# A planner's model of one PSUM bank: when a transposition into the shared bank counts as ready

## The chip, the cores and the metric

The kernel runs on one core of a Trainium2 chip. The metric is the device time of one execution in microseconds (us); the runs shown are executions of the same program. PE is TensorE, DVE is VectorE, ACT is ScalarE, POOL is GpSimd, SP is SyncE.

## The reference, cut to what matters

Three layers follow each other on the same 3072 tokens of width 512.

```
x  = attention(q, k, v)            # 4 x 8 heads, 768 tokens, local window of 96 and 8 global keys
x  = x + gate * moe(x)             # tokens with x @ w_skip > 0; expert = argmax(x @ w_gate); probability as gate
    h = max(x[mask] @ w1[e], 0);  y[mask] = gate * (h @ w2[e])       # 8 experts, 512 -> 1024 -> 512
out = moe2(x)                      # each expert takes at most 384 tokens, greedily over all sorted logits
    for idx in argsort(-logits.flatten()): take the token for the expert if both are still free
    h = max(x[mask] @ w1[e], 0);  out[mask] = h @ w2[e]
```

## The kernel before

After the attention (until about 238 us) come two series of expert products. In the first, one unit is one expert with 256 token slots (two blocks of 128), eight units, and one extra unit for an expert with too many tokens. In the second, one unit is one expert with 384 slots (three blocks), again eight units. Before a unit's products its token rows are gathered from memory by slot numbers (tile xg), turned block by block by four 128x128 transpositions on PE into the PSUM tile pt (`x_turn`, line 1044), copied by ACT as the rounded half xh, and subtracted on DVE for the remainder xl (`x_low`, line 1054). A product is done as three rounded ones (xh with wh, xl with wh, xh with wl). `mm1` (line 1058) makes ph = x @ w1 for one eighth of the hidden width, 12 matmuls; ACT and DVE make hh and hl of it; `mm2` (line 1083) adds h @ w2 into py, 9 matmuls in the second series. Weights come from memory (wr), ACT rounds them (wh), POOL or DVE subtracts (wl).

All tiles named pt share one PSUM bank: the pool `fps` (line 1022) has one buffer per name. Five places write one: the turns of x, the epilogue of the first series (`tr`, line 1281, which turns the result rows x2), the extra unit (`extra_rest`, line 1469), and two small products of the slot numbers (`slots`, line 1686: pb and pi).

Beside the expert products run generators, called streams: the turns of the next unit ("x"), the routing of the second layer ("main", which finds a threshold by counting in rounds of DVE comparisons gm and PE products pr), its slot numbers ("ids"), and the extra unit ("extra"). The program is written out in one order per engine while it is built, and that order is chosen by a model of the engines, `Clock` (line 20): each instruction written is given a start and an end from the model's costs, and the model remembers who wrote and read which part of each tile. A stream yields the engine it goes on with and the tiles that it reads. Before each expert matmul `hook` (line 1151) asks each stream in order of rank whether it is ready by the time PE gets there:

```
t = max(ck.at["pe"] + T_EPS, ck.ready("pe", (), aps))
for s_ in order():
    if s_.when() <= t:
        s_.step()
```

`when` (line 1141) is the model's time at which the tiles to be read are written. `wait_for` (line 1162) steps the streams until a condition holds, where nothing else is to be written. In `x_stream` (line 1178) the subtraction of a turn is put on a list (`lows`) and written to DVE when xh is there in the model (`flush`, line 1174); the next turn is asked for right after that. A unit's start waits for all its turns (`split2`, line 1195). "x" has rank 3 until the routing is more than a unit ahead, then rank 0, "main" 2 and then 1, "ids" 0.5 and then 2, "extra" 4.

In the model a DVE subtraction of 128x512 costs 0.067 + 512/960 us, and a result of DVE reaches PE 0.15 us after its end. Line 123 is the helper through which all instructions are written, so all carry it in the profile.

Of the kernel before, what the change touches and what calls it, by code (L numbers as in the profile page):

```python
# [7 lines left out]
F32 = mybir.dt.float32  # L8
# [153 lines left out]
def tile_attn_moe_moe(ctx: ExitStack, tc: tile.TileContext, q, k, v, n_global, n_local,  # L162
# [12 lines left out]
    KC = Dm // 128  # L175
# [348 lines left out]

    WWT, WWN = 1, (2, 5)
    T_GAP, T_SP, T_EPS, T_W, T_P, T_L, T_F, X_B, T_H, T_M, LEAN, T_G, DIRECT, CUT = 0, 0.65, 0.1, 0, 8, 1, 0.3, 3, -4, 0, 2, 1, 13, 16
    ck.late = T_G
    W_ = Weights()

# [324 lines left out]
    class Unit:  # L854
        at, tb, py, defer, xh = None, 0, 0, None, None
# [10 lines left out]
    for e in range(E):  # L866
        U_ = Unit()
# [154 lines left out]
    fps = ctx.enter_context(tc.tile_pool(name="fps", bufs=1, space=bass.MemoryType.PSUM))  # L1022
# [4 lines left out]
    bank = fps.tile([128, 512], I32, name="bank")  # L1027
    bank_at = [192]

    def in_bank(n, dt=F32):  # L1030
        bank_at[0] += n
        return bank[:, bank_at[0] - n:bank_at[0]].bitcast(dt)
# [8 lines left out]
    raw_p, fe_p = in_bank(NT), in_bank(NT)  # L1041
    fo_p = in_bank(2 * E).rearrange("p (a e) -> p a e", a=2)

    def x_turn(U_, tb, bank="pt"):
        if tb == 0 and not U_.xh:
            U_.xh = ff.tile([128, KC, width], F32R, name="xh")
            U_.xl = ff.tile([128, KC, width], F32R, name="xl")
        p = fps.tile([128, KC, 128], F32, name=bank)
        for c in range(KC):
            nc.tensor.transpose(p[:, c], U_.xs[tb][:, c * 128:(c + 1) * 128], ident)  # L1050
        U_.xt[tb] = p
        nc.scalar.activation(U_.xh[:, :, tb * 128:(tb + 1) * 128], p, AF.Copy)
# [75 lines left out]
    class Stream:  # L1128
# [11 lines left out]

        def when(self):
            eng, aps = self.need
            t = ck.ready(eng, (), aps)
            return max(t, ck.at["dve"] - T_SP) if eng == "dve" else t

# [26 lines left out]
    lows = []  # L1172

    def flush():
        while lows:
            lows.pop()()

    def x_stream(U_):
        for tb in range(len(U_.xs)):
            yield "pe", [U_.xs[tb]]  # L1180
            x_turn(U_, tb)
            lows.append(lambda tb=tb: x_low(U_, tb))
            yield "dve", [U_.xh[:, :, tb * 128:(tb + 1) * 128]]
            flush()
            U_.tb += 1
# [82 lines left out]
    def epi1(U_, tasks):  # L1268
        nb = len(U_.xs)
        if U_.defer is not None:  # L1270
            if U_.defer == 0:
                tasks.append(lambda: gate2(U_))
                tasks.append(lambda: gate2_rows(U_))
                tasks.append(table)
                tasks.extend([lambda: None] * 3)
                tasks.append(table_clear)
            return
        rows2(U_)
        U_.x2t = fx_.tile([128, KC, 256], F32, name="x2t")

        def tr(tb):
            flush()
            p = fps.tile([128, KC, 128], F32, name="pt")
            for c in range(KC):
                nc.tensor.transpose(p[:, c], U_.x2[tb][:, c * 128:(c + 1) * 128], ident)
            nc.scalar.activation(U_.x2t[:, :, tb * 128:(tb + 1) * 128], p, AF.Copy)

        def lg():
            p = fps.tile([128, 256], F32, name="pr")
            n = nb * 128  # L1290
            for c in range(KC):
                nc.tensor.matmul(p[c * 32:(c + 1) * 32, :n], wg2[:, c, :], U_.x2t[:, c, :n], start=True, stop=True)
            U_.ls = fx_.tile([128, 256], F32, name="ls1")
            nc.scalar.activation(U_.ls[:, :n], p[:, :n], AF.Copy)

        def lt():
            p = fps.tile([128, HI, KC, 32], F32, name="pr")
            for tb in range(nb):
                nc.tensor.transpose(p[:, tb].rearrange("p c e -> p (c e)"), U_.ls[:, tb * 128:(tb + 1) * 128], ident)
            lgo = ff.tile([128, HI, E], F32, name="lgo")  # L1300
            nc.vector.tensor_reduce(lgo[:, :nb], p[:, :nb, :, :E].rearrange("p j c e -> p j e c"),
                                    axis=AX.X, op=OP.add)
            for tb in range(nb):
                scatter(l2d, U_.sid[:, tb:tb + 1], lgo[:, tb], l2_st)
            U_.tasks = None

        U_.tasks = tasks
        for tb in range(nb):
            tasks.append(lambda tb=tb: tr(tb))
        tasks.append(lg)  # L1310
        tasks.append(lt)
        if U_ is not X_:
            tasks.extend(rt_tasks[:3])
            del rt_tasks[:3]
# [20 lines left out]
    tb_rhs = rt.tile([128, NT + 3], BF, name="tb_rhs")  # L1335
# [133 lines left out]
    def extra_rest(hs_):  # L1469
        hT = []  # L1470
        for half in range(2):
            yield "pe", hs_[2 * half:2 * half + 2]
            flush()
            p = fps.tile([128, 4, 128], F32, name="pt")
            for c in range(4):
                nc.tensor.transpose(p[:, c], hs_[2 * half + c // 2][:, c % 2 * 128:(c % 2 + 1) * 128], ident)
            th = fx_.tile([128, 4, 128], F32R, name=f"th{half}")
            tl_ = fx_.tile([128, 4, 128], F32R, name=f"tl{half}")
            nc.scalar.activation(th, p, AF.Copy)
            nc.vector.tensor_tensor(tl_, p, th.bitcast(F32), op=OP.subtract)  # L1480
            hT.append((th, tl_))
            X_.turned += 1
        X_.y = [fps.tile([128, Dm], F32, name="py2")]
        for c in range(FC):
            need(NE * NCH + 4 + c // 2)
            ww = W_.parts[NE * NCH + 4 + c // 2]
            for i, (a, b_) in enumerate(P3):
                yield "pe", [hT[c // 4][a], ww[b_]]
                nc.tensor.matmul(X_.y[0], hT[c // 4][a][:, c % 4], ww[b_][:, (c % 2) * Dm:(c % 2 + 1) * Dm],
                                 start=c == 0 and i == 0, stop=c == FC - 1 and i == 2)  # L1490
            W_.free = 4 * NE + (c + 1) // 2
            W_.pump()
        while units1[NE - 1].tasks:
            units1[NE - 1].tasks.pop(0)()
        tasks = []
        epi1(X_, tasks)
        for ap, t in zip((X_.x2[0], X_.x2t, None), tasks):
            yield "pe", [ap if ap is not None else X_.ls]
            t()
# [186 lines left out]
    def slots(ph_, fe, fx):  # L1686
        ttb = rt.tile([128, 1], BF, name="ttb")
        dv.tensor_tensor_scan(fe[:, 5], fe[:, 4], wrow_p[:, :NT], 0.0, op0=OP.add, op1=OP.bypass)
        dv.tensor_copy(ttb, fe[:, 5, NT - 1:NT])
        dv.tensor_copy(tb_rhs[:, :NT], fe[:, 5])  # L1690
        yield "pe", [ttb]
        flush()
        pb = fps.tile([128, KC, 128], F32, name="pt")
        te(pb[:, 0, 0:1], tri, ttb, start=True, stop=True)
        dv.tensor_copy(fx[:, 3:4], pb[:, 0, 0:1])
        dv.tensor_tensor(fx[:, 4:5], pb[:, 0, 0:1], fe[:, 5, NT - 1:NT], op=OP.add)
        dv.tensor_scalar(tb_rhs[:, NT + 1:NT + 2], fx[:, 3:4], 256.0, None, op0=OP.min)
        ma = rt.tile([128, CAP], F32, name="ma")
        mp = rt.tile([128, CAP], BF, name="mp")
        dv.tensor_scalar(ma, islot, fx[:, 3:4], None, op0=OP.is_ge)  # L1700
        dv.tensor_tensor(tb_rhs[:, NT + 2:NT + 3], pb[:, 0, 0:1], tb_rhs[:, NT + 1:NT + 2], op=OP.subtract)
        dv.scalar_tensor_tensor(mp, islot, fx[:, 4:5], ma, op0=OP.is_lt, op1=OP.mult)
        yield "pe", [mp, tb_rhs]
        flush()
        pi = fps.tile([128, KC, 128], F32, name="pt")
        for h in range(NH):
            te(pi[:, h, :NT + 3], mp[:, h * 128:(h + 1) * 128], tb_rhs, start=True, stop=True)
        ix = rt.tile([128, 3, NH], F32, name="ix")
        cx = rt.tile([128, NH, NT], F32, name="cx")
        ids = rt.tile([128, NH], I32, name="ids", bufs=E)  # L1710
        dv.tensor_tensor(ix[:, 0], snum, pi[:, :NH, NT + 1], op=OP.subtract)
        dv.tensor_tensor(ix[:, 0], ix[:, 0], pi[:, :NH, NT + 2], op=OP.subtract)
        dv.tensor_tensor(cx, pi[:, :NH, :NT], ix[:, 0][:, :, None].to_broadcast([128, NH, NT]), op=OP.is_le)
        dv.tensor_reduce(ix[:, 1], cx, axis=AX.X, op=OP.add)
        dv.scalar_tensor_tensor(ids, pi[:, :NH, NT], float(NT), ix[:, 1], op0=OP.mult, op1=OP.add)
        result[ph_] = ids
        if ph_:
            if unit_no[0] >= ph_ - 1:
                units2[ph_].load()
# [39 lines left out]
    for p in range(E):  # L1759
        U_ = Unit()  # L1760
# [62 lines left out]
```

## Time and profile before

| what | us |
|---|---|
| median of 3 runs | 870.54 (867.64 to 871.69) |
| the profiled execution | 866.52 |
| its span, first to last instruction | 864.8 |
| PE busy (matmuls) in the span | 772.2 |
| PE weight loads busy | 629.1 |
| DVE, ACT, POOL busy | 522.2, 411.4, 422.1 |

The mean granted clock of PE is 0.959 of 2.4 GHz. In the profile a row names engine, operation, output<-inputs by tile names; "idle before" is the time in which the engine stood still just ahead of an instruction, and behind the arrow is what ended that. Ends of matmuls are modelled, since they are pipelined: one that lies in a stream of others starts before the one ahead has ended. PEld rows are the weight loads of PE.

### The profile page before, as it was taken

What the parts mean: (1) busy time and instruction counts of PE and PEld (TensorE: products, weight loads), DVE (VectorE), ACT (ScalarE), POOL (GpSimd) and SP (SyncE); (2) the same over time, 40 slices, a digit from 0 to 9 for tenths busy, and PEclk for the clock granted to TensorE, in tenths of its full rate; (3) what the DMA queues carried; (4) which work ended last, traced back from release to release, by engine and by line L of the source; (5) the groups of instructions that cost most, each with busy time, mean ns of one, the idle gap of its engine ahead of it and who ended that gap; (6) DMA issues with size and microseconds to landing.
All of it is one profiled execution on the core that took longest, in us unless ns stands there. A gap on an engine that the chain in (4) does not pass through costs nothing.

```text
span 864.8 us, 16657 instructions
## 1 busy us (share of the span) xinstructions
PE 772.2 (89%) x5711; PEld 629.1 (73%) x5711; DVE 522.2 (60%) x1896; ACT 411.4 (48%) x923; POOL 422.1 (49%) x569
## 2 busy tenths in 40 slices
PE   7999998998788899998879938998989898899994
PEld 5777776676577778787768626777778787798993
DVE  6978879795555555644443584777777777712110
ACT  5887787875465445543552123334243342435211
POOL 5554557643234335442341444566484847568411
PEclk9999999999979999998999965999999999999997
DMA  8677888877166466545550051526263443555000
GB/s 188 178 207 184 231 213 218 223 208 217 28 195 206 155 213 212 189 143 183 170 192 6 17 203 49 168 89 219 91 202 116 154 135 134 161 180 164 32 37 36
DMA packets 141013, 132.82 MB, mean 154 GB/s; under 512 B 62523, under 2 KB 107835, under 8 KB 140928
## 3 DMA queue, kind: packets, MB, share of 16 engines
q1 hardware_dynamic: 132160, 111.09, 43.1%
q0 software_dynamic: 7168, 20.26, 6.8%
q8 instruction: 46, 0.75, 0.4%
q10 hardware_dynamic: 1600, 0.39, 0.2%
q14 instruction: 39, 0.32, 0.1%
HBM read 109.55 MB, written 23.49 MB: 154 GB/s over the span
## 4 chain that ended last, share of the span: by engine, by line
PE 41%; issue 11%; DVE 9%; POOL 4%; DMA 3%; ACT 2%; POOLq 0%; SPq 0%; DVEq 0%; ACTq 0%
PE ph L123 19%; PE py L123 17%; PE pr L123 3%; DMA wr<-in_moe_w_dram 3%; PE pt L123 3%; POOL wl L123 2%; DVE bank L123 2%; ACT wh L123 1%; DVE gm L123 1%; DVE xl L123 1%; DVE wl L123 1%; POOL out_dram L123 1%; DMA xg<-xd,gid 1%; DVE hl L123 1%; DVE fr L123 0%
## 5 line engine op out<-in xcount | busy, mean ns | idle before, releaser
L123 POOL TENSOR_TENSOR wl<-wr,wh 128x1024 fp32r<-128x1024 f32 (+1 forms) x97 | 204.8, 2128 | 143.6 <-ACT wh L123 142.9
L123 ACT ACTIVATE wh<-wr 128x1024 fp32r<-128x1024 f32 (+1 forms) x148 | 141.1, 984 | 49.2 <-PE py L123 27.5
L123 ACT ACTIVATE hh<-ph 128x384 fp32r<-128x384 f32 (+2 forms) x130 | 56.7, 436 | 224.5 <-PE ph L123 202.5
L123 DVE SCALAR_TENSOR_TENSOR hl<-ph,hh 128x256 fp32r<-128x256 f32 (+1 forms) x128 | 62.3, 487 | 129.8 <-ACT hh L123 124.4
L123 PE MATMUL py<-wh,hl 128*128 128x512 f32 x320 | 129.4, 404 | 1.6 <-DVE hl L123 1.6
L123 PE MATMUL py<-wh,hh 128*128 128x512 f32 x320 | 128.6, 402 | 0.4 <-ACT hh L123 0.4
L123 PE MATMUL py<-wl,hh 128*128 128x512 f32 x320 | 128.9, 403 | 0.0
L123 POOL TENSOR_SCALAR pb<-pb,st 128x232 f32<-128x232 f32 (+1 forms) x192 | 82.4, 448 | 72.5 <-PE pP L123 25.6
L123 ACT ACTIVATE pb<-sb,st 128x232 f32<-128x232 f32 (+1 forms) x192 | 113.8, 663 | 4.8 <-DVE st L123 4.5
L123 PE MATMUL ph<-xh,wh 128*128 128x256 f32 (+1 forms) x512 | 106.0, 325 | 2.5 <-ACT wh L123 1.5
L123 PE MATMUL ph<-xl,wh 128*128 128x256 f32 (+1 forms) x512 | 102.8, 319 | 0.0
L123 PE MATMUL ph<-xh,wl 128*128 128x256 f32 (+1 forms) x512 | 102.4, 319 | 0.0
L123 PEld LDWEIGHTS ph<-xh,wh 128*128 128x128 f32 x512 | 84.4, 194 | 12.1 <-issue 2.3
L123 PEld LDWEIGHTS ph<-xl,wh 128*128 128x128 f32 x512 | 82.4, 194 | 0.2
L123 PEld LDWEIGHTS ph<-xh,wl 128*128 128x128 f32 x512 | 81.9, 194 | 0.4 <-issue 0.2
L123 DVE TENSOR_TENSOR wl<-wr,wh 128x1024 fp32r<-128x1024 f32 x51 | 64.6, 1287 | 24.3 <-ACT wh L123 23.6
L123 PEld LDWEIGHTS py<-wh,hl 128*128 128x128 f32 x320 | 60.7, 190 | 14.0 <-DVE hl L123 2.4
L123 DVE COPY pts<-pP 116x512 f32<-116x512 f32 (+1 forms) x96 | 61.0, 676 | 13.0 <-PE pP L123 12.2
L123 PEld LDWEIGHTS py<-wh,hh 128*128 128x128 f32 x320 | 60.9, 190 | 8.0 <-ACT hh L123 0.6
L123 PEld LDWEIGHTS py<-wl,hh 128*128 128x128 f32 x320 | 60.8, 190 | 8.0
L123 DVE CUSTOM_DVE_ANT_0 sb<-pS,bias 128x232 f32<-128x232 f32 (+1 forms) x192 | 61.4, 373 | 2.0 <-PE pS L123 1.4
L123 ACT ACTIVATE xh<-pt 128x512 fp32r<-128x512 f32 x38 | 22.7, 597 | 60.4 <-PE pt L123 48.4
(454 smaller groups left out, 1220.0 us busy)
## 6 DMA issues: line engine op xcount, KB each, us to landing
wr<-in_moe_w_dram SPq DMA_DIRECT2D x136, 512.0 KB
xd<-xs SPq DMA_DIRECT2D x32, 192.0 KB
x2d<-xs SPq DMA_DIRECT2D x32, 192.0 KB
kraw<-in_k_dram SPq DMA_DIRECT2D x30, 192.0 KB
qraw<-in_q_dram SPq DMA_DIRECT2D x30, 192.0 KB
vw<-in_v_dram SPq DMA_DIRECT2D x32, 160.0 KB
vw<-in_v_dram SPq DMA_DIRECT2D x32, 120.0 KB
xT<-in_moe_w_dram SPq DMA_DIRECT2D x1, 1536.0 KB
```

The costliest lines, as they stand in the source:

```text
L123: r = f(*a, **k)
```

## The change

For four of the five writers the stream now says "pt" instead of "pe". For those, `when` also asks the model for the time at which the last pt tile written has been read by all who read it, and adds 0.7 us if a subtraction that reads it has still to be written. The tile is remembered in `last_pt` by a helper `turns()`. Tile, bank, pool and the instructions themselves are as before.

```
+    T_LOW = 0.7
+    last_pt = []
+    def turns():
+        p = fps.tile([128, KC, 128], F32, name="pt")
+        last_pt[:] = [p[:, :, :]]
+        return p
     def x_turn(U_, tb, bank="pt"):
-        p = fps.tile([128, KC, 128], F32, name=bank)
+        p = fps.tile([128, KC, 128], F32, name=bank) if bank != "pt" else turns()
         def when(self):
             eng, aps = self.need
+            if eng == "pt":
+                return ck.ready("pe", last_pt, aps) + (T_LOW if lows else 0)
             t = ck.ready(eng, (), aps)
             return max(t, ck.at["dve"] - T_SP) if eng == "dve" else t
     def x_stream(U_):
         for tb in range(len(U_.xs)):
-            yield "pe", [U_.xs[tb]]
+            yield "pt", [U_.xs[tb]]
         def tr(tb):
             flush()
-            p = fps.tile([128, KC, 128], F32, name="pt")
+            p = turns()
     def extra_rest(hs_):
-            yield "pe", hs_[2 * half:2 * half + 2]
+            yield "pt", hs_[2 * half:2 * half + 2]
-            p = fps.tile([128, 4, 128], F32, name="pt")
+            p = turns()
     def slots(ph_, fe, fx):
-        yield "pe", [ttb]
+        yield "pt", [ttb]
-        pb = fps.tile([128, KC, 128], F32, name="pt")
+        pb = turns()
-        yield "pe", [mp, tb_rhs]
+        yield "pt", [mp, tb_rhs]
-        pi = fps.tile([128, KC, 128], F32, name="pt")
+        pi = turns()
```

## Rows read from the trace of the kernel before

**Rows 1.** Busy time by stage: stretch, its length, busy per engine (instructions), PEclk, DMA.
```profile
238.00:500.00 262.00, 238.21 (x1613) 201.12 (x1614) 132.66 (x263) 115.03 (x180) 98.81 (x105) 0.96 0.46 155
500.00:525.00 25.00, 8.17 (x99) 5.97 (x98) 17.91 (x60) 6.78 (x9) 9.88 (x10) 0.57 0.55 196
525.00:800.00 275.00, 259.24 (x1565) 212.68 (x1565) 177.88 (x736) 104.56 (x150) 174.63 (x113) 0.97 0.45 145
```

**Rows 2.** Waits of PE from 525 to 800 us: total, times, longest.
```profile
PE pt L123 <- DVE xl L123: 12.4, 12, 1.2
PE pt L123 <- issue: 1.7, 2, 1.2
PE pt L123 <- DVE mp L123: 1.6, 1, 1.6
```

**Rows 3.** Waits of PE from 238 to 500 us.
```profile
PE pt L123 <- DMA xg<-xd,gid: 4.9, 5, 1.3
PE pt L123 <- DVE tl L123: 4.7, 2, 3.3
PE pt L123 <- DVE xl L123: 2.9, 4, 0.9
...
PE ph L123 <- ACT wh L123: 1.5, 1, 1.5
PE pt L123 <- ACT x2t L123: 1.4, 2, 0.7
PE pt L123 <- issue: 1.1, 1, 1.1
```

**Rows 4.** Timeline of PE, 558 to 561 us: start, length, instruction [idle before].
```profile
558.32 0.39 PE L123 MATMUL py<-wl,hh 128*128 128x512 f32 x1
558.55 0.39 PE L123 MATMUL py<-wh,hl 128*128 128x512 f32 x1
560.16 0.66 PE L123 MATMUL pt<-ident,xg 128*128 128x128 f32 x4 [1.22 <-DVE xl L123]
560.65 0.30 PE L123 MATMUL pr<-oh,gm 128*128 128x32 bf16 x6
```

**Rows 5.** Timeline of DVE in the same stretch.
```profile
558.95 0.56 DVE L123 SCALAR_TENSOR_TENSOR hl<-ph,hh 128x384 fp32r<-128x384 f32 x1
559.42 0.68 DVE L123 TENSOR_TENSOR xl<-pt,xh 128x512 fp32r<-128x512 f32 x1
```

**Rows 6.** Groups of weight loads, 525 to 800: count, busy, mean ns, idle before.
```profile
L123 PEld LDWEIGHTS pt<-ident,xg 128*128 128x128 f32 x84 | 9.3, 140 | 20.1 <-DVE xl L123 17.1 <-issue 2.4
```

**Rows 7.** Groups of matmuls from 525 to 800 us, the same columns.
```profile
L123 PE MATMUL pr<-oh,gm 128*128 128x32 bf16 x180 | 9.3, 178 | 0.0
L123 PE MATMUL pr<-cs,sel 128*128 128x32 f16 x30 | 5.7, 189 | 0.0
```

**Rows 8.** Timeline of PE at the extra unit, 421 to 425.5 us.
```profile
422.73 0.39 PE L123 MATMUL ph<-xh,wh 128*128 128x256 f32 x1 [1.46 <-ACT wh L123]
...
424.97 0.68 PE L123 MATMUL pt<-ident,hh 128*128 128x128 f32 x2 [1.41 <-DVE tl L123]
```

**Rows 9.** Busy time by stage again, around the two falls of the clock.
```profile
391.00:397.70 6.70, 6.00 (x26) 5.50 (x27) 1.24 (x2) 2.11 (x5) 1.59 (x2) 0.50 0.72 243
425.00:428.40 3.40, 3.40 (x10) 2.86 (x11) 1.41 (x2) 2.29 (x3) 1.14 (x1) 0.50 0.84 247
388.00:391.00 3.00, 0.00 (x0) 0.00 (x0) 1.83 (x2) 2.04 (x3) 1.85 (x2) 0.98 1.02 391
```

**Rows 10.** Timeline at the start of unit 1, DVE and PE.
```profile
568.77 0.68 DVE L123 TENSOR_TENSOR xl<-pt,xh 128x512 fp32r<-128x512 f32 x1
...
574.39 0.86 PE L123 MATMUL ph<-xl,wh 128*128 128x384 f32 x4
```

**Rows 11.** Timeline of PE ahead of unit 0, second and third turn.
```profile
519.12 1.09 PE L123 MATMUL pt<-ident,xg 128*128 128x128 f32 x4 [1.13 <-issue]
...
522.84 1.09 PE L123 MATMUL pt<-ident,xg 128*128 128x128 f32 x4 [2.52 <-issue]
```

## The prediction, on record before the result

> **What bounds the kernel now.** I read the page's busy shares first, then the busy time by stage, then what TensorE (PE) waited for in each stage, then single instructions in order of time.
>
> The stages [rows 1] show PE busy 238.2 of 262 us in the first matrix products, and 259.2 of 275 us in the first seven units of the second. Between them lie 25 us of routing in which PE works 8.2 us. DVE is busy 178 and POOL 175 of the 275 us: neither is near full. The reader is to see that outside the short stage nothing but PE itself, and what PE stands still for, can set the time.
>
> What PE stood still for from 525 to 800 us is one thing [rows 2]: 12.4 us in 12 stops until the subtraction "xl" on DVE, 1.7 us in 2 more at the same instruction that the view puts down to issue, and 1.6 us for the routing's own "mp". So 14 stops, 14.1 us, all ahead of a transposition into the bank pt: the second and third turn of each of seven units. From 238 to 500 us the list is longer [rows 3]: at pt again 2.9 us in 4 stops for xl and 1.1 us in one; 4.7 us in 2 for "tl" (the longest 3.3); 1.4 us in 2 for the copy x2t; and 4.9 us in 5 for gathered rows that had not landed.
>
> One stop from close by [rows 4]: the py matmul starts at 558.55, the next instruction of PE, four transpositions of a second turn, at 560.16. On DVE [rows 5] hl runs from 558.95 and xl, the last reader of the bank, from 559.42 to 560.10. The planner let the turn go as soon as its rows were there; PE reached it and stood. Behind it in PE's order were matmuls with everything they need.
>
> **The change part by part.** No instruction is added or removed: it alters the moment at which a generator that is about to write pt counts as ready. Four places ask that way: a turn of x, the extra unit's two turns, and two small products of the slot numbers. The epilogue's turns (tr) only report their bank and aren't asked.
>
> *Turns in the second matrix products.* 14 stops of 14.1 us go [rows 2]. The column of idle time undercounts: the py before starts 0.23 us after its forerunner (558.32, 558.55), so PE could have gone on at 558.78; it went on at 560.16, 1.38 us later, where the column has 1.22 [rows 4]. That is 0.16 us more per stop, 14 x 0.16 = 2.2 us. Cover: mm1 and mm2 are asked before every matmul, and a unit's 168 of them in the expert products stand ready, since rows 2 show no wait of theirs. If that cover were gone, the stop would be back at 1.0 us on the mean.
>
> The weight loads of these turns stood 17.1 + 2.4 = 19.5 us [rows 6] where the matmuls stood 14.1. The Trainium skill ("Perfetto Trace Analysis", section Identifying the Most-Contended Engine) says that the busy time of matmuls is a poor measure of PE, as they are pipelined, and that weight loads are to be looked at instead. By that rule alone this stage would give 5.4 us more than the column, and the sum below 3.2 us more; the trace agrees in direction, and my size is that of the starts.
>
> *Turns in the first matrix products.* From rows 3 go xl 2.9 us, issue 1.1 us, one of the two x2t stops (a turn of x right behind a turn of tr), 0.7 us, and one of the two tl stops, the extra unit's second turn, 1.4 us: 6.1 us in 7 stops, with 7 x 0.16 = 1.1 us more. The other tl stop (3.3 us) and the other x2t stop are tr's and stay; the gathers' 4.9 us stay too, since what the planner thinks of a landing isn't altered.
>
> *Is the planner right about DVE?* If it lets the turn go too early, part of the stop stays. Lower bound nothing: other instructions that the same model lets go when DVE is done, 180 + 30 of the routing's products, show 0.0 us of idle time in all [rows 7]. Upper bound: where the model is wrong, as with the gathers, 4.9 / 5 = 1.0 us is left per stop [rows 3], which is all of it. The routing's products are nearer: same stage, same pair of engines. The formula has 0.067 + 512/960 = 0.60 us for xl and 0.15 us for the hand-over; measured are 0.68 us [rows 5] and 0.06 us (560.10 to 560.16), so 0.75 against 0.74. I still take 0.15 us per stop, about a matmul's pitch: 21 x 0.15 = 3.2 us off. T_LOW, 0.7 us, stands for an xl not yet issued and is the measured length.
>
> *Cover at the extra unit.* At 422.73 PE had waited 1.46 us for weights and at 424.97 it waits 1.41 us for tl [rows 8]: little else is ready there. From nothing to 1.4 us can come back as a wait for weights; I take half, 0.7 us.
>
> *The clock.* Behind two stops of PE the granted clock was 0.50, the lower level: 391 to 397.7 us, after three empty microseconds, and 425 to 428.4 us, after the two stops of rows 8 [rows 9]. At half clock those cost 6.7/2 = 3.4 and 3.4/2 = 1.7 us. The second may go with its stop, the first keeps its cause (tr's). Nothing to 1.7 us gained (up to 5.1 should both go); I take nothing.
>
> *What moves.* Each deferred turn waited on PE for this same subtraction, so it starts no earlier and at most a matmul or two later. Unit 1 has the least room: its last xl begins at 568.77 and ends at 569.45, its first matmul with xl starts at 574.39 [rows 10], 4.9 us later. With 2 x 1.38 us saved ahead of it 2.1 us are left; cost nothing, and one for one beyond. What stood behind a stopped turn, such as the routing's products at 560.65 [rows 4], comes up to 1.4 us sooner; not counted. Ahead of unit 0 (515 to 525 us) two stops of 1.1 and 2.5 us [rows 11] have no expert product that could fill them, only the routing: 1 us either way, taken as nothing. The slot products write pt tens of microseconds from the turns, except the last two units'; nothing, or one turn's delay of about 3.7 us (519.12 to 522.84) with room to spare. The queues of SP and POOL get the same issues in the same order as far as the routing isn't overtaken; the gathers are issued before the turns.
>
> *Sum.* 14.1 + 2.2 + 6.1 + 1.1 - 3.2 - 0.7 = 19.6 us less. The profiled execution took 866.5 us (864.8 us of span and 1.7 around it), so 846.9. It ran 4.0 us under the median of the runs, 870.5; against that median I forecast 870.5 - 19.6 = 850.9 us.
>
> **Rivals.**
> *The first half gives it back.* With PE 1 us sooner in each unit of the first product, it meets weights, gathers and hl. For it: the 1.46 us for weights [rows 8] and the gathers [rows 3]. Against: in 262 us rows 3 have one wait for weights. Then only the second half counts: 14.1 + 2.2 - 14 x 0.15 = 14.2, time 856.3; with half of that lost too, 863.
>
> *It doesn't do what it says.* The model's PE or DVE runs ahead of the real ones and the turn still comes too soon, as for the gathers. Then the stops stay at 1.0 us and the time is 867 to 872. Against it: rows 7.
>
> *Slower: the turns starve.* While a turn isn't ready, the routing and the slot numbers go, and their DVE work then stands ahead of the next xl, as hl does in rows 5. Should the last two turns slip to the unit's start, they run with no matmul beside them, 3.7 us each as ahead of unit 0 [rows 11], 7.4 us of an empty PE, and by rows 9 a stretch at the lower clock behind it, 3.4 us: 10.8 us a unit. It decides from the point where the last xl passes the unit's first matmul, 4.9 us in unit 1 [rows 10]; two units would cancel the gain (21.6 against 19.6), three make it 850.9 + 32.4 = 883 us. For it: the deferral is repeated for every turn. Against it: once a unit's slot numbers are there the turns have rank 0, ahead of all others, and a deferral is one subtraction long.
>
> **How the numbers follow.** The forecast has 0.72, with a range of its own from 844 (both clock dips gone, no residue: 5.1 + 3.2 us more would be 842.6; I go most of the way) to 855. The half gain has 0.15, no effect 0.07, slower 0.06. From 844 to 863 the range holds nearly all of the first and most of the second, 0.83. A measurement of this kernel can tell about 0.5%, 4.4 us, from no change: faster 0.87, the same 0.07, slower 0.06.
>
> **What would show it.** Right: in the second products the waits of PE for xl fall from 12.4 us to under 3 with equal busy time; the turn's transpositions stand between two matmuls of one group with no idle time; the stage from the first ph of unit 0 to the end shrinks by about 14 us, the first product by about 6. The clock at 425 us tells of that dip. Wrong: stops of 1.0 us still ahead of pt; new waits at ph or py for xl, hl or wh; PE empty at a unit's start with turns back to back.

## The result, and the profile after

The changed kernel takes 846.8 us (median of 4 runs, 843.7 to 848.3) against 869.7 us for the kernel before: a ratio of 0.975, 95% interval 0.972 to 0.978. A second measurement on another chip gave 0.973 (0.970 to 0.977). The forecast was 850.9 us, within 844 to 863.

The waits of PE from 525 to 800 us, the stretch of [rows 2], are the shortest proof. Columns: total, times, longest.

```profile
PE pt L123 <- DVE tb_rhs L123: 2.9, 1, 2.9
PE pr L123 <- DVE fl L123: 0.2, 1, 0.2
PE pr L123 <- DVE ei L123: 0.2, 1, 0.2
```

All 14 stops until xl are gone, and the 1.6 us for mp with them. One stop of 2.9 us is new; it has a section of its own below. In the first series, the stretch of [rows 3]:

```profile
PE pt L123 <- DMA xg<-xd,gid: 6.6, 5, 2.0
PE pt L123 <- DVE tl L123: 3.3, 1, 3.3
...
PE ph L123 <- ACT wh L123: 1.5, 1, 1.5
PE ph L123 <- DVE xl L123: 0.9, 1, 0.9
...
PE pt L123 <- ACT x2t L123: 0.7, 1, 0.7
...
PE pt L123 <- DVE xl L123: 0.6, 2, 0.4
```

Stops for xl at pt fell from 2.9 + 1.1 to 0.6 us, and those for tl and x2t lost one stop each. The gathers wait longer, 6.6 for 4.9 us, and 0.9 us for xl is new at ph, at the start of one unit: PE comes sooner, and these things are sooner by less.

A turn now, unit 1's second and third, PE and then DVE in order of time (start, length; [rows 4, 5] are the turn before):

```profile
554.72 0.39 PE L123 MATMUL py<-wh,hh 128*128 128x512 f32 x1
554.95 0.60 PE L123 MATMUL pt<-ident,xg 128*128 128x128 f32 x4
555.30 0.47 PE L123 MATMUL py<-wl,hh 128*128 128x512 f32 x1
...
558.19 0.60 PE L123 MATMUL pt<-ident,xg 128*128 128x128 f32 x4
```

```profile
553.95 0.68 DVE L123 TENSOR_TENSOR xl<-pt,xh 128x512 fp32r<-128x512 f32 x1
557.24 0.68 DVE L123 TENSOR_TENSOR xl<-pt,xh 128x512 fp32r<-128x512 f32 x1
```

xl ends at 554.63 and the turn starts at 554.95, between two matmuls of one group with their usual 0.23 us, not at the head of an empty PE. The second xl ends at 557.92, its turn starts at 558.19. In these two the planner lets the turn go 0.3 us after the bank is free: the error lies on the harmless side.

Busy time by stage splits the gain. Columns: stretch, length, PE, weight loads, DVE, ACT, POOL busy (instructions), granted clock, DMA share, GB/s. The stretches run from the first ph of the first series to the first ph of the second, from there to the end, and over the half-clock beginning of the second. First the kernel before, then the changed one.

```profile
242.60:524.60 282.00, 244.01 (x1701) 205.23 (x1701) 149.13 (x317) 119.92 (x186) 106.84 (x114) 0.94 0.48 161
524.60:864.80 340.20, 312.14 (x1829) 260.04 (x1826) 184.87 (x749) 116.56 (x170) 189.78 (x130) 0.96 0.38 124
524.60:541.10 16.50, 16.50 (x117) 12.31 (x115) 7.83 (x28) 5.66 (x7) 10.66 (x5) 0.50 0.09 34
```

```profile
246.20:521.70 275.50, 241.62 (x1703) 204.45 (x1703) 150.38 (x321) 119.68 (x186) 108.81 (x113) 0.95 0.49 165
521.70:845.90 324.20, 308.51 (x1825) 260.37 (x1825) 186.11 (x746) 116.61 (x170) 189.95 (x130) 0.96 0.41 130
521.70:533.10 11.40, 11.40 (x80) 9.04 (x81) 5.57 (x17) 3.70 (x6) 5.56 (x3) 0.50 0.18 48
```

The expert products of the first series by themselves, from the first ph to the last py, before and then after, and the changed kernel's first fall of the clock in them ([rows 9] has that of before, 6.7 us):

```profile
242.60:501.40 258.80, 237.64 (x1610) 200.49 (x1611) 132.65 (x267) 114.13 (x178) 96.96 (x104) 0.97 0.47 157
246.17:499.42 253.25, 235.00 (x1610) 199.62 (x1611) 133.39 (x267) 113.89 (x178) 98.70 (x103) 0.98 0.48 160
393.20:396.60 3.40, 3.38 (x15) 2.92 (x15) 0.88 (x2) 1.40 (x4) 0.46 (x2) 0.50 0.88 283
```

The first stage is 6.5 us shorter, the second 16.0: together 22.5 us. (This execution entered the first series 3.6 us later than that of before, behind the attention, in which nothing was changed; so its span is only 18.9 us shorter, while the medians differ by 22.9.) Of the 6.5 us, 5.6 (258.80 to 253.25) are the first series itself and 1.0 the routing between the two. In the second stage PE's idle time fell by 12.4 us, 28.1 to 15.7: 14.1 us of stops and mp's 1.6, less the new 2.9 and 0.4 of small ones. Its busy time fell by 3.6 us with the same work: half clock lasted 11.4 us and not 16.5, worth 5.1/2 = 2.5 us, against 1.7 us lost behind the new stop; the remaining 2.8 us, found by subtraction alone, are put down to what the column of idle time leaves out.

### The profile page after: what moved, and what is told of

Same layout as the page of the kernel before. It is cut to its first block, busy times and chain, and to the rows that moved or that the text cites. A ratio compares the mean times of both kernels' runs of the same rounds, so it can differ in the third digit from the quotient of the medians.

```text
span 845.9 us, 16662 instructions
## 1 busy us (share of the span) xinstructions
PE 768.8 (91%) x5711; PEld 631.0 (75%) x5711; DVE 525.4 (62%) x1896; ACT 411.8 (49%) x923; POOL 425.0 (50%) x569
## 4 chain that ended last, share of the span: by engine, by line
PE 31%; issue 20%; POOL 11%; DVE 4%; DMA 3%; ACT 1%; another core or an unknown queue 0%; POOLq 0%; DVEq 0%
PE ph L123 14%; PE py L123 13%; POOL wl L123 6%; PE pr L123 3%; POOL out_dram L123 2%; PE pt L123 2%; DMA xg<-xd,gid 1%; DMA wr<-in_moe_w_dram 1%; POOL xg L123 1%; DVE bank L123 1%; POOL x2d L123 1%; ACT wh L123 1%; POOL l2d L123 1%; DVE wl L123 0%; DVE fe L123 0%
## 5 line engine op out<-in xcount | busy, mean ns | idle before, releaser
L123 PE MATMUL ph<-xh,wl 128*128 128x256 f32 (+1 forms) x512 | 104.3, 321 | 0.0
L123 PEld LDWEIGHTS py<-wh,hl 128*128 128x128 f32 x320 | 60.5, 189 | 14.2 <-DVE hl L123 2.4
L123 PE MATMUL pP<-ident,pb 128*116 128x128 f32 (+1 forms) x384 | 51.7, 278 | 0.0
```

The lines of the kernel that those rows point to most:

```text
L123: r = f(*a, **k)
```

## The new stop: DVE waits for POOL

Timeline of the changed kernel around 735 us on DVE, then on POOL:

```profile
735.40 0.16 DVE L123 TENSOR_SCALAR tb_rhs<-fx 128x1 bf16<-128x1 f32 x1
735.48 4.43 DVE L123 TENSOR_SCALAR ma<-islot,fx 128x384 f32<-128x384 f32 x1
739.83 0.14 DVE L123 TENSOR_TENSOR tb_rhs<-pt,tb_rhs 128x1 bf16<-128x1 f32 x1
```

```profile
734.96 4.71 POOL L123 TENSOR_TENSOR wl<-wr,wh 128x1024 fp32r<-128x1024 f32 x2
```

ma takes 0.41 us in five of its seven other places in the same execution (0.47 and 1.31 in the two left) and 4.43 us here; it ends 0.24 us after POOL's second wl. The next DVE operation is the last reader of the bank, so unit 6's first turn stood 2.93 us on PE, and the clock was 0.50 from 741.4 to 744.7 us. The Trainium skill ("SBUF — State Buffer", section SBUF: two separate sides) says that a DVE operation in a two-port mode or with two SBUF inputs and one of GpSimd exclude each other for a whole instruction. The trace agrees in that ma ended only behind POOL's work, and shows more: it got through only after two POOL operations that followed each other without a pause.

The stop is new, what makes it isn't. In the kernel before, the copy tb_rhs (0.17 us at its shortest) took 2.21 us and ended with a wl, on DVE and POOL:

```profile
738.95 2.21 DVE L123 CAST tb_rhs<-fe 128x24 bf16<-128x24 f32 x1
```

```profile
738.73 2.40 POOL L123 TENSOR_TENSOR wl<-wr,wh 128x1024 fp32r<-128x1024 f32 x1 [7.63 <-ACT wh L123]
```

The 1.6 us for mp in [rows 2] stand 2.6 us behind it, at 743.78, in the same chain of slot numbers. This waiting of DVE for POOL is called "the port" below.

## The experiments

All ratios are to the kernel before, timed on the same chip in the same session. Sessions were on different chips; differences between them of 0.004 decide nothing.

**Which of the four askers matters.** x_only:

```
-            yield "pt", hs_[...] / [ttb] / [mp, tb_rhs]
+            yield "pe", ...        # extra unit and slot numbers as before; x_stream keeps "pt"
```

> Only the turns of x ask for the bank; the extra unit's turns and the slot numbers ask for their inputs alone, as before. Theory (the gain is the stops of x's turns that go): all but the extra unit's stop of 1.4 us is theirs, so the time is 847 to 850 us, a ratio of 0.974 to 0.979 to the kernel before. Rival (the slot numbers, moved past the bank, bring the routing forward and that is the gain): a good part of the 22 us is lost, over 855 us.

Measured: 843.1 us, ratio 0.976 (0.970 to 0.982): the ratio as expected, the time below it, since the kernel before, timed beside it, took 865.2. The whole gain is there with x's turns alone. Without their own asking, the slot numbers' product stands 1.4 us once, at 735.1 until a turn's xl, which is too little for these times to tell.

**Which series.** second_only: as x_only, and in `x_stream`:

```
-            yield "pt", [U_.xs[tb]]
+            yield "pt" if width == CAP else "pe", [U_.xs[tb]]
```

> Only the turns of x in the second series ask for the bank. Theory: the stops of the first series are back (2.9 + 1.1 + 1.4 + 0.7 us and the part that the column leaves out), so 5 to 7 us of the gain is lost: 852 to 854 us, ratio 0.980 to 0.982; PE waits for xl about 3 us from 238 to 500 us and under 1 us after. Rival (the first series meets its weights and gathers sooner and gives its part back): no loss, 846 to 849 us.

Measured: 849.7 us, ratio 0.9815 (0.977 to 0.986): again the expected ratio at a lower time. PE's waits at pt in the first series:

```profile
PE pt L123 <- DVE tl L123: 4.7, 2, 3.3
PE pt L123 <- DVE xl L123: 3.1, 3, 1.6
```

The stops for x's turns are back there and only there. Beside x_only, which differs in nothing else and was timed with it, the first series is worth 849.7 - 843.1 = 6.6 us by the medians, and 0.0053 x 865 = 4.6 us by the middles of the two ratios; the intervals overlap, so times alone don't settle it. The profile's 5.6 us for the first series says the same: it did not give its part back.

**Stop or order.** early: the same planner, its time for the bank 0.6 us too early.

```
-                return ck.ready("pe", last_pt, aps) + (T_LOW if lows else 0)
+                return max(ck.ready("pe", (), aps), ck.ready("pe", last_pt, aps) + (T_LOW if lows else 0) - 0.6)
```

> The model's time for the bank is taken 0.6 us too early. Theory (what counts is how long PE stands at the bank): up to 0.6 us of each of 21 stops is back, 0.4 to 0.6 on the mean as a turn goes a little after its time anyway, so PE waits 6 to 10 us for xl and the time is 852 to 858 us. Rival (what counts is the order, the routing being let past; a stop of half a microsecond vanishes in slack elsewhere): 846 to 849 us.

Measured: 855.1 us, ratio 0.985 (0.981 to 0.990); about half of the gain is lost. PE's waits from 525 to 800 us:

```profile
PE pt L123 <- DVE mp L123: 4.3, 1, 4.3
PE pt L123 <- DVE xl L123: 3.0, 10, 0.4
PE pt L123 <- issue: 0.8, 2, 0.4
```

Twelve stops of 0.3 us on the mean are back in the second series and two, 1.3 us, in the first: 5.1 us, under the expected 6 to 10. (The waits until xl and those put down to issue come to 7.1 us over the whole kernel, but 1.9 of them lie ahead of unit 0.) That the gain shrinks where the stops come back, with all else of the change in place, speaks for the stop as the price. Not all of the loss is theirs: mp's 4.3 us is the port again (mp lasted 5.60 us, its shortest 0.62) and 1.4 us more than the stop it replaces, and unit 0 has 16.2 us at half clock, against 11.4 in the changed kernel.

**Too late.** late adds 3 us instead; late_x adds them for x alone; late_port is late with the PSUM operands of the run port (below).

```
+                return ... + 3.0                          # late, late_port
+                return ... + 3.0 * (self.kind == "x")     # late_x
```

> The model's time for the bank is taken 3 us too late, for each turn. Theory (the turns have slack to their unit's start, 5 us at unit 1 and 8 or more after it; PE has other matmuls meanwhile): two deferrals of 3 us cost about 1 us at unit 1 and up to 3 us each at unit 7 of the first series, where the last turn is already waited for, and ahead of unit 0 of the second, where PE has nothing else: 848 to 855 us. Rival (turns starve: each unit's last turns slip to its start with nothing beside them, and the clock falls): 10 us a unit, over 865 us.

Measured: 890.9 us, ratio 1.029 (1.023 to 1.034): slower than before, and against my theory, which had 848 to 855. But not by the rival's way either; PE doesn't stand for turns at the units' starts in the main. Its waits from 525 to 860 us:

```profile
PE pr L123 <- DVE ei L123: 12.1, 4, 4.4
PE pr L123 <- DVE cs L123: 8.7, 4, 4.5
PE pr L123 <- DVE gm L123: 8.2, 5, 3.1
PE pt L123 <- DVE xl L123: 8.2, 3, 5.3
```

Most are the routing's. Its DVE operations between SBUF tiles in that stretch (count, busy, mean ns), which take 0.17 us (c, tb_rhs), 0.41 (ma) and 0.62 (mp) at their shortest:

```profile
L123 DVE CAST c<-fe 128x2 bf16<-128x2 f32 x5 | 13.1, 2621 | 0.2
L123 DVE SCALAR_TENSOR_TENSOR mp<-islot,fx,ma 128x384 bf16<-128x384 f32 x7 | 11.1, 1591 | 0.0
L123 DVE TENSOR_SCALAR ma<-islot,fx 128x384 f32<-128x384 f32 x7 | 9.1, 1305 | 0.0
L123 DVE CAST tb_rhs<-fe 128x24 bf16<-128x24 f32 x6 | 8.7, 1445 | 0.0
```

A copy of two elements per partition takes 2.6 us on the mean. So there were two candidates for the rest: the port, and the slot numbers, which defer twice a phase and for which the next phase waits.

> The bank's time 3 us too late, as in the run late, with the PSUM operands of the run port. Theory (late is slow because its routing steps fall on POOL's work: DVE operations 36 us longer than their shortest, PE standing 29 us ahead of the routing's products): most of that goes, 855 to 868 us. Rival (late is slow because turns starve): it stays over 880 us.

Measured: 869.1 us, ratio 1.002 (0.999 to 1.005), just above the expected 855 to 868. None of those operations is lengthened any more, and 0.027 x 868 = 23 us are gone: about half of what late lost against the changed kernel. The rest is not the port.

> The 3 us too late for the turns of x alone; the slot numbers and the extra unit ask as in the changed kernel. Theory (late lost its time through the slot numbers: each phase of the routing waits for them, two deferrals a phase, and the routing then comes too late for the units and onto POOL's work; x's own turns have their slack): 845 to 852 us, ratio 0.974 to 0.982. Rival (x's turns themselves starve at the units' starts): over 865 us, ratio over 0.995, with PE waiting at ph for xh and xl.

Measured: 848.7 us, ratio 0.977 (0.975 to 0.979). x's own turns can come 3 us late at a cost of 0.002 to 0.004, no more than sessions differ. So nearly all of late's loss, 1.029 against 0.977, hangs on deferring the slot numbers (or the extra unit's two turns, not tried apart), and about half of it goes through the port. The small cost of late_x is a sum: its routing between the series lasts 31.1 us and not 22.2, and its first series 248.8 us and not 253.2, with no stop left for gathered rows. The starving of x's turns, my slower rival, isn't a danger at 3 us.

**Taking the port away.** port: ma lies in the free columns of the bank pt, the two running sums behind c and tb_rhs in another PSUM bank; one small operation a phase is added.

```
-        ma = rt.tile([128, CAP], F32, name="ma")
+        ma = pb[:, 1:1 + NH].rearrange("p a n -> p (a n)")
-            sc, g1 = fe[:, 2:4], fe[:, 1]
+            sc, g1 = sc_p, fe[:, 1]                     # sc_p, cum_p: columns of the PSUM tile bank
-        dv.tensor_tensor_scan(fe[:, 5], ...)
+        dv.tensor_tensor_scan(cum_p, ...)               # and its three readers
```

> The changed kernel, with the DVE operations of the slot numbers that had all their operands in SBUF given one in PSUM (ma goes to the bank pt, two running sums to another bank; one small DVE operation of 0.17 us more a phase). Theory (a DVE operation between SBUF tiles stands still as long as POOL works: ma at 735.5 us took 4.43 us instead of 0.41 and ended when POOL's second wl ended): ma, c and tb_rhs take 0.2 to 0.6 us everywhere in the second series, PE's stop of 2.9 us until tb_rhs and the lower clock behind it (3.4 us long) are gone, 3 to 5 us less than the changed kernel. Rival (ma waited for the bank or for a semaphore): it is as long as before, and the time is that of the changed kernel or 1 us more.

> The changed kernel itself, beside the three others. Ratio to the kernel before 0.972 to 0.978, as measured for it.

Measured together: the changed kernel 844.0 us, 0.973 (0.970 to 0.977); port 839.4 us, 0.968 (0.964 to 0.972), 4.5 us less; the intervals just overlap, and the profile decides. Its DVE groups, and all of PE's waits from 525 to 800 us:

```profile
L123 DVE TENSOR_SCALAR pt<-islot,fx 128x384 f32<-128x384 f32 x8 | 4.9, 610 | 0.0
L123 DVE CAST tb_rhs<-bank 128x24 bf16<-128x24 f32 x8 | 1.4, 173 | 0.0
L123 DVE CAST c<-bank 128x2 bf16<-128x2 f32 x7 | 1.1, 160 | 0.2
```

```profile
PE pr L123 <- DVE fl L123: 0.2, 1, 0.2
```

ma is dearer by itself, 0.61 us, and never waits. PE stands still 0.2 us in 275.

**The other stops at the bank.** land_x: the landing of gathers 1.3 us later in the model during the first series; the extra unit's turn waits until the epilogue's turns are through; a pending subtraction is written ahead of the next turn.

```
-    ck.late = T_G
+    ck.late = 2.3                     # T_G again from the second series on
         def when(self):
+            if self.kind == "extra" and getattr(units1[NE - 2], "tasks", None):
+                return ck.at["pe"] + 100.0
     def x_stream(U_):
             yield "pt", [U_.xs[tb]]
+            flush()
```

> The changed kernel, with the model's landing of gathered rows 1.3 us later in the first series, and the extra unit's turn held until the epilogue's turns are through. Theory (the same kind of stop at the same bank, of other causes): PE's 6.6 us for gathered rows fall under 2, the 3.3 us for tl goes with the lower clock behind it (3.4 us long): 7 to 11 us less than the changed kernel. Rival (the turns then come late for their units): PE waits for xh or xl at ph instead, and the time is the same within 3 us.

Measured beside the two above: 837.8 us, ratio 0.966 (0.962 to 0.969), 6.2 us under the changed kernel, a little short of 7 to 11. Waits of PE in the first series:

```profile
PE pt L123 <- issue: 2.5, 2, 2.1
...
PE pt L123 <- DMA xg<-xd,gid: 1.6, 3, 0.6
```

The gathers' 6.6 us fell to 1.6 and tl's 3.3 us is gone, but 2.5 us put down to issue stand at pt: 2.05 of them at 392.8, ahead of the turn of the extra unit's own gathered rows, and 0.48 at a turn of x. What ended them the trace doesn't show.

**Both.** all: port and land_x.

> The edits of port and of land_x together. Theory (they take away different stops, 2.9 us and its dip of the clock here, gathers and tl there): their gains over the changed kernel add, 4.5 + 6.5 = 11 us: ratio 0.960 to 0.963, 832 to 836 us. Rival (PE then meets weights or the routing): no better than land_x alone, 0.966.

Measured: 833.4 us (831.2 to 835.0), ratio 0.959 (0.957 to 0.961). The gains add, and this version beats both kernels: 4.1% less than the kernel before, with 0.2 us of waits of PE from 525 to 800 us.

## Why the prediction was right, step by step

Of the 22.5 us between the two profiles about 4.9 came from the clock, less 1.7 lost behind the new stop; the forecast of 19.6 had the clock at nothing. The mechanism held, and that the size came so near is in part luck.

- *That only PE and what it stands for set the time.* Right, with the clock as a third. In the stages read here, changes of PE's idle time came through to the time; neither weights nor POOL took over, with POOL busy 190 us of the second stage before and after.
- *Second series, 14.1 + 2.2 - 2.1 = 14.2 us.* Measured 16.0. The 14 stops went entirely, so the 2.1 us that I held back for a planner that is wrong had no ground: it errs by 0.3 us towards late. The 2.2 us from the starts came as 2.8 of busy time, by subtraction; 14.1 + 2.8 = 16.9 us lies by the starts' 16.3 and not by the 19.5 of the weight loads. The rest is two things I had not counted, of opposite sign: unit 0 ran 5.1 us less at half clock (2.5 us), and the new stop with its fall of the clock cost 2.9 + 1.7, less mp's 1.6 us. Without the clock in unit 0 the stage would have given 13.5.
- *The clock in unit 0* was no term of mine. Unit 0 had 16.5 us at half clock before and 11.4 after; in the second profile of the changed kernel it had 5.4 us, and 3.4 more at 528.5. The same program differs by that much, and x_only, port and all lie between (9.5 to 10.3), while early has 16.2 and second_only 11.4 and 3.4 more. So it tends to be less with the change, in one profile of each kernel and two of the changed one; why is not shown.
- *First series, 6.1 + 1.1 - 1.1 - 0.7 = 5.4 us.* Measured 5.6 for the first series, and 1.0 for the routing behind it, which I had taken as nothing. That 5.6 is so near is luck: terms that failed cancel. Stops of 5.5 us went (xl left 0.6 us and not 1.1, and nothing came back at the extra unit). But the gathers took back 1.7 us and one late turn 0.9, where I had them unchanged and nothing, so PE's idle time fell by 2.9 us only. The term "the gathers' 4.9 us stay" failed: counted from the first ph, the last of these rows landed 4.8 us sooner, and PE came for them 5.7 us sooner. (In x_only, whose turns of x are planned alike, PE waited 2.7 us for them, so this part scatters.) The other 2.6 us are busy time, and about 2.4 of it is the clock: half clock lasted 3.6 us for 5.1 at the start of the series and 3.4 us at 393 for 6.7. So little of the 1.1 us from the starts can be seen here.
- *Extra unit and clock.* The stop of 1.41 us went whole (I kept half of it). The fall of the clock at 425 us went too, but one of the same length stood at 434. The fall at 391, which I had said keeps its cause, was half as long, worth 1.7 us; in the second profile it is missing (1.00 from 385 to 400 us), with the same stop of 3.3 us for tl ahead of it. So that stop alone doesn't settle the clock, and my "nothing" for it was too little in both.
- *The half gain given back.* Refuted by second_only and by the stage, though 2.6 of the 5.5 us in stops did come back as other waits. *It doesn't do what it says*: refuted by the waits.
- *Turns starve.* Hardly: one unit's start, the last of the first series, waited 0.9 us for its last xl; and late_x shows that they would bear 3 us. What would have made this change slower is another asker: the slot numbers, which I had put down as "nothing, or one turn's delay of about 3.7 us" with room to spare. At the change's own setting that held (x_only is no faster); at 3 us the room is gone, and the port, which no part of the prediction had though the trace before shows it at 738.95, doubles the loss.

## What to carry to other kernels

Where a program is put in order by a model, an idle gap that repeats ahead of one instruction is a resource the model doesn't know; teach it that, and the gap fills from work that stands ready. Price such a gap by the starts of the instructions on either side, and look in the new trace for DVE operations far longer than the shortest of their kind, for a shifted order can lay them onto POOL's work.

## What the runs showed of the hardware

Some DVE operations whose tensors all lie in SBUF stand as long as POOL works: ma 4.43 instead of 0.41 us across two wl of 2.4 us, and in the run late a copy of 128x2 that took 4.63 us, beginning just behind a wl and ending when two were through:

```profile
592.89 4.63 DVE L123 CAST c<-fe 128x2 bf16<-128x2 f32 x1
```

```profile
592.84 4.64 POOL L123 TENSOR_TENSOR wl<-wr,wh 128x1024 fp32r<-128x1024 f32 x2
```

Not all such operations do. Ten reductions and operations on one element per partition that began and ended while a wl ran in late took 0.16 to 0.49 us, as elsewhere; one of the kind is tb_rhs<-fx at 735.40 in the lines of the new stop. Those seen to stand in these runs are the copies of 2 and 24 elements, ma and mp.

With a source or a result in PSUM, the same steps in the runs port, late_port and all took 0.16 to 0.61 us each time, and 21 of them began and ended while a wl ran, as here in late_port:

```profile
727.69 0.61 DVE L123 TENSOR_SCALAR pt<-islot,fx 128x384 f32<-128x384 f32 x1
```

```profile
727.24 4.76 POOL L123 TENSOR_TENSOR wl<-wr,wh 128x1024 fp32r<-128x1024 f32 x2 [0.35 <-ACT wh L123]
```

Whether a gap between POOL's operations would let DVE in wasn't tried. POOL's issue of an indirect transfer may hold DVE too: early's mp began at 737.56, while POOL issued one (737.11 to 738.06) and 0.5 us ahead of the next wl, and ended at 743.16. This too wasn't tried by itself.
